# Left queries of two batches gathered in one late stage, keys turned over two PSUM banks, and one pair of heads divided after its product

## The chip, the cores and the metric

The kernel runs on one core of one Trainium2 chip. The metric is the device time of one execution in microseconds (us). The core has five engines that run side by side: TensorE (PE in the profile: matmuls and transposes, results in PSUM), VectorE (DVE), ScalarE (ACT), GpSimd (POOL) and SyncE (SP), whose queue issues nearly all DMAs. PSUM has eight banks of 512 float32 columns on 128 partitions.

## The reference

Eight batches, eight heads, 576 rows, head size 64; then a maxout feed-forward over the 4608 x 512 result. All in float32 (the weights arrive as float64).

```
q_s = exp(q - max over head size);  q_s = q_s / (sum over head size + 1e-9)
k_s = exp(k - max over rows);       k_s = k_s / (sum over rows + 1e-9)
kv  = k_s^T @ v                     # 64 x 64 for each batch and head
a   = q_s @ kv                      # 576 x 64
x   = a of all heads side by side   # 4608 x 512
h   = max(x @ w1, x @ w2, x @ w3)   # 4608 x 768
out = h @ w_out                     # 4608 x 512
```

## The kernel before

**Tiling.** Heads go in pairs (four pairs g per batch, pair number n = 4 b + g), so that two heads fill 128 partitions. Of the 576 rows of a head, 512 are its main rows and 64 are "left"; main rows of one batch make a chunk (c = 0 to 7), and the left rows of all batches together make the ninth chunk (c = 8), whose input is the tile `left`. A float32 product of full precision is made from three fast ones on high and low parts (`wh`, `wl`, `oh`, `ol`, `x` with two halves, `h_h`, `h_l`).

**Weights.** They come as 24 slices of 512 KB (18 for the gates, 6 for w_out). A `Slice` is loaded (L332), its float64 words are joined into float32 by DVE, ACT and POOL (L342 to L359), and split into a high part (L363, ACT) and a low part (L370, DVE or POOL). Four slices are among the first loads. Of the others, every second one from number 8 on is loaded into buffers that open with the event "late".

**Attention, batches 0 and 1 ("turned").** `k_turned` transposes the keys of a pair on PE: four blocks into a tile `pa` (a bank of three), the left block into a quarter of the tile `ps` (one bank, four quarters). DVE takes the maxima of both parts (L450, L451) and their smaller (L452), ACT the exponentials with their sums (L456, L457), PE transposes back (L464, L466), and two copies give `ke` (L473). `k_steps` multiplies keys and values (L511) into a quarter of `ps`, and ACT scales the result into `bdf`, one of two buffers (L527). `q_steps` takes the maxima of ten groups of 64 columns (L550: eight of main rows, two of left rows), then either ten exponentials of 64 columns with their sums (`Q_BY_ACT`, pairs 0 to 6, L567) or one subtraction and one exponential, and scales by the sums (L595). `turned_steps` transposes main rows (L636) and left rows (L640) and copies both to `qf` (L645, L647). `x_steps` multiplies `bdf` by `qf` for main rows and for left rows (L663) and splits the results into high (L666, ACT) and low (L668, DVE).

**Attention, batches 2 to 7.** `k_plain` takes the maximum over rows on GpSimd, the queries are turned by DVE and DMAs, and the products are made in three passes. These start with the event "turn", when all slices are split and batch 1 is done. `x_steps` runs for main and left rows here too.

**Feed-forward.** For each chunk 18 gates (`Chunk.gate`, L693: four column blocks `cc`, one from each pair, three matmuls each), maxima and split (`Chunk.hidden`, L702 to L712), then four output tiles of 18 matmuls (`Chunk.second`, L732). A gate's block `cc` needs x of pair g = cc and one weight slice. The four gate tiles `pf` take half of PSUM.

**Order.** Nothing is looped in plain order: each of these is a generator of steps, each step with an engine, a cost, what it needs and what it frees, and `Streams` plays them against a clock per engine. On an engine it takes, of the steps that could begin, the one of lowest rank, and emits instructions in that order; every engine then runs its own list strictly in order. The ranks come from constants: `AT` and `STEP` (pairs of batches 0 and 1), `FIRST` and `CHUNK` (the later batches), `SLICES_AT`, `SLICE`, `SLICE_STEP`, `SLICE_HI` and `SLICE_LO` (weights), `GATES_AT` (gates). `FIRST_LOADS` spells the first DMAs: w a slice, k, q, v the main rows of the next pair of batch 0, and the capital letters the left rows (the first time those of pair 0, the second time those of pairs 1 to 3). The event "late" is given by

```python
yield Step("-", 0.0, [(x, 0, g) for x in ("x", "xl") for g in range(NP)], gives="late")
```

Of the kernel before, what the change touches and what calls it, by code (L numbers as in the profile page):

```python
# [42 lines left out]
Q_BY_ACT = (0, 1, 2, 3, 4, 5, 6)  # L43
# [6 lines left out]
def dve_reduce(n):  # L50
    return (n + 140) / 960
# [28 lines left out]
class Streams:  # L80
# [88 lines left out]
    def issue(self, t, e, c, s):  # L169
        step = s[4]  # L170
        end = t + c
# [24 lines left out]
def linear_attention_then_maxout_ffn(  # L196
# [49 lines left out]
    pa = ctx.enter_context(tc.tile_pool(name="pa", bufs=3, space=PSUM))  # L246
    ps = ctx.enter_context(tc.tile_pool(name="ps", bufs=1, space=PSUM))
# [16 lines left out]
    q0 = early.tile([P, H, 5, D], F32, name="q0")  # L264
    v0 = early.tile([P, H, 5, D], F32, name="v0")
    bdf = [start.tile([P, P], F32, name=f"bdf{i}", bufs=1) for i in range(2)]
    qbuf = [start.tile([P, 2, 5, D], F32, name=f"q1{i}", bufs=1) for i in range(2)]
# [14 lines left out]
    nc.gpsimd.memset(q0[LEFT:P, :, 4, :], 0.0)  # L282
    for i in range(2):
        nc.gpsimd.memset(bdf[i], 0.0)
    for i in range(2):
        nc.gpsimd.memset(qbuf[i][LEFT:P, :, 4, :], 0.0)
        nc.gpsimd.memset(vbuf[i][:, :, :, D:NV], 1.0)
        nc.gpsimd.memset(vbuf[i][LEFT:P, :, 4, :], 0.0)
# [13 lines left out]
    st = Streams({"pf": 4, "pa": 3, "ps": 4, "keT": 1, "hp": NJ, "tmp": 3, "ke": 2, "qe": 2, "qf": 1, "qt": 2, "tb": 1, "qT": 2, "qhl": 1}, {"pf": in_pf})  # L302
    late_pools, turn_pools = [], []

    quarters = ps.tile([P, 4, P], F32, name="ps")
    small = (quarters[:, i % 4, :] for i in itertools.count())
# [67 lines left out]
    class Pair:  # L374


        def __init__(self, b, g):
            self.b, self.g = b, g
            self.hs = slice(2 * g, 2 * g + 2)
            self.n = b * NP + g  # L380
            self.m = self.n % 2
            self.turned = b < TURNED
            if b == 0:
                self.kt, self.vt, self.qt = k0[:, :, self.hs], v0[:, self.hs], q0[:, self.hs]
            else:
                self.kt, self.vt = kbuf[self.m], vbuf[self.m]
                if self.turned:
                    self.kt = self.kt.rearrange("p h s d -> p (h s d)").rearrange("p (s h d) -> p s h d", s=5, h=2)

# [19 lines left out]
        def v_load(self):  # L409
            if self.b:  # L410
                prev = self.ago("kv") if self.n >= NP + 2 else None
                for hh in range(2):
                    yield Step("S", 0.64, [prev], kb=200)
                    nc.sync.dma_start(out=self.vt[:, hh, 0:4, 0:D], in_=head_rows(v, self.b, 2 * self.g + hh))
# [3 lines left out]
        def q_load(self):  # L418
            if self.b == 0:
                return  # L420
            if self.turned:
                prev = self.ago("qsub") if self.n >= NP + 2 else None
                self.qt = qbuf[self.m]
                yield Step("S", 0.64, [prev], kb=256)
                nc.sync.dma_start(out=self.qt[:, :, 0:4, :], in_=main_rows(q, self.b, self.hs))
                yield Step("S", 0.64, gives=("q", self.n), kb=50)
                nc.sync.dma_start(out=self.qt[0:LEFT, :, 4, :], in_=left_rows(q, self.b, self.hs))
# [6 lines left out]
        def k_turned(self):  # L434

            n, kt = self.n, self.kt
            rooms = [("pa", ("kT", n)), ("ps", ("kTl", n))]
            yield Step("T", 0.6, [("k", n)], take=rooms + [("keT", n)], gives=("ksub", n))
            kT = pa.tile([P, CH], F32, name="pa")
            for s in range(4):  # L440
                nc.tensor.transpose(  # L441
                    out=kT[:, s * P : (s + 1) * P], in_=kt[:, s].rearrange("p h d -> p (h d)"), identity=ident
                )
            kTl = next(small)
            nc.tensor.transpose(
                out=kTl[:, :LEFT], in_=kt[:LEFT, 4].rearrange("p h d -> p (h d)"), identity=ident[:LEFT, :LEFT]
            )
            yield Step("V", dve_reduce(CH) + dve_reduce(LEFT) + 0.13)
            km = att.tile([P, 2], F32, name="km2", bufs=4)
            nc.vector.tensor_reduce(out=km[:, 0:1], in_=kT, op=ALU.max, axis=AX.X, negate=True)  # L450
            nc.vector.tensor_reduce(out=km[:, 1:2], in_=kTl[:, :LEFT], op=ALU.max, axis=AX.X, negate=True)  # L451
            nc.vector.tensor_tensor(out=km[:, 0:1], in0=km[:, 0:1], in1=km[:, 1:2], op=ALU.min)  # L452
            yield Step("A", act(CH) + act(LEFT) + 0.2, free=rooms)
            keT = start.tile([P, S], F32, name="keT", bufs=1)
            ks = self.ks = att.tile([P, 2], F32, name="ks", bufs=4)
            nc.scalar.activation(out=keT[:, :CH], in_=kT, func=AF.Exp, bias=km[:, 0:1], accum_out=ks[:, 0:1])  # L456
            nc.scalar.activation(  # L457
                out=keT[:, CH:], in_=kTl[:, :LEFT], func=AF.Exp, bias=km[:, 0:1], accum_out=ks[:, 1:2]
            )
            rooms = [("pa", ("ke", n)), ("ps", ("kel", n))]  # L460
            yield Step("T", 0.6, take=rooms + [("ke", n)], free=[("keT", n)])
            kep = pa.tile([P, CH], F32, name="pa")
            for s in range(4):
                nc.tensor.transpose(out=kep[:, s * P : (s + 1) * P], in_=keT[:, s * P : (s + 1) * P], identity=ident)  # L464
            kel = next(small)
            nc.tensor.transpose(out=kel[:LEFT, :], in_=keT[:, CH:], identity=ident)  # L466
            e = yield Step("AV", (act(CH) + act(P), dve(CH) + dve(P)), free=rooms)
            ke = self.ke = att.tile([P, 5, 2, D], F32, name="ke")
            for o, i in (
                (ke[:, 0:4].rearrange("p s h d -> p (s h d)"), kep),  # L470
                (ke[:LEFT, 4].rearrange("p h d -> p (h d)"), kel[:LEFT, :]),
            ):
                (nc.scalar.copy if e == "A" else nc.vector.tensor_copy)(out=o, in_=i)  # L473
# [24 lines left out]
        def k_steps(self):  # L498
# [5 lines left out]
                "T", 0.9, [("v", n), self.ago("xmm", 0), self.ago("xmm", 1)], take=last, free=[("ke", n)], gives=("kv", n)  # L504
# [12 lines left out]
            if turned:  # L517
                nc.vector.tensor_scalar(
                    out=rk, in0=self.ks[:, 0:1], scalar1=self.ks[:, 1:2], scalar2=1e-9, op0=ALU.add, op1=ALU.add
                )  # L520
# [4 lines left out]
            for r in heads:  # L525
                to = (bdf if turned else bdh)[self.m]
# [14 lines left out]
        def q_steps(self):  # L541
            n = self.n
            rows = 10 if self.turned else QS
            by_act = n in Q_BY_ACT
            qm = att.tile([P, rows], F32, name=f"qm{rows}", bufs=4)
            qs = att.tile([P, rows], F32, name=f"qs{rows}", bufs=4)
            yield Step("V", dve_reduce(rows * D), [("q", n)])
            if self.turned:
# [4 lines left out]
                if by_act:  # L553
                    yield Step("A", 5 * 0.33, take=[("qe", n)])
# [4 lines left out]
                qe = self.qe = start.tile([P, 5, 2, D], F32, name="qe", bufs=2)  # L559
                rows3 = qe.rearrange("p s h d -> p (s h) d")  # L560
                sums = qs.rearrange("p (s h) -> p s h", h=2)
                if by_act:
                    for hh in range(2):
                        if hh:
                            yield Step("A", 5 * 0.33, gives=("qsub", n))
                        for s in range(5):
                            nc.scalar.activation(  # L567
                                out=qe[:, s, hh, :], in_=src[:, hh, s, :], func=AF.Exp,
                                bias=qm[:, 5 * hh + s : 5 * hh + s + 1], accum_out=sums[:, s, hh : hh + 1],
                            )  # L570
                else:
# [3 lines left out]
                        in1=qm.rearrange("p (h s) -> p h s", h=2).unsqueeze(3).broadcast_to([P, 2, 5, D]),  # L575
                        op=ALU.subtract,
                    )
            else:
# [5 lines left out]
                )  # L584
            if not by_act:
# [4 lines left out]
            yield Step("V", 0.34)  # L590
# [39 lines left out]
        def turned_steps(self):  # L630

            n = self.n
            yield Step("T", 0.5, [("qn", n)], take=[("qf", n), ("pa", ("qT", n)), ("ps", ("qTl", n))], free=[("qe", n)])
            qT = pa.tile([P, CH], F32, name="pa")
            for s in range(4):
# [3 lines left out]
            qTl = next(small)  # L639
            nc.tensor.transpose(  # L640
                out=qTl[:, :LEFT], in_=self.qe[:LEFT, 4].rearrange("p h d -> p (h d)"), identity=ident[:LEFT, :LEFT]
            )
            e = yield Step("AV", (act(CH), dve(CH)), free=[("pa", ("qT", n))])
            qf = start.tile([P, S], F32, name="qf", bufs=1)
            (nc.scalar.copy if e == "A" else nc.vector.tensor_copy)(out=qf[:, :CH], in_=qT)  # L645
            yield Step("A", act(LEFT), free=[("ps", ("qTl", n))], gives=("qhl", n))
            nc.scalar.copy(out=qf[:, CH:], in_=qTl[:, :LEFT])  # L647
            self.terms = [(bdf[self.m], qf)]

        def x_steps(self, u):  # L650
# [4 lines left out]
            cost = f32(w) if self.turned else 3 * f32r(w)  # L655
# [3 lines left out]
            yield Step("T", cost, after, take=[room], gives=("xmm", n, u), free=[("qf" if self.turned else "qhl", n)] if u else ())  # L659
            xT = (next(small) if u else pa.tile([P, CH], F32, name="pa"))[:, :w]  # L660
            last = len(self.terms) - 1
            for i, (l, r) in enumerate(self.terms):
                nc.tensor.matmul(out=xT, lhsT=l, rhs=r[:, cs], start=(i == 0), stop=(i == last))  # L663
# [4 lines left out]
            nc.vector.tensor_sub(out=lo, in0=xT, in1=h.bitcast(F32))  # L668

    class Chunk:
# [6 lines left out]
        def gate(self, j, i):  # L679
            c, js = self.c, slice(j * P, (j + 1) * P)  # L680
            key = (c, j, i)
            for cc in range(NC):
                x = [("x", c, cc)] if c < B else [("xl", b, cc) for b in range(B)]
# [240 lines left out]
```

## Time and profile before

| what | us |
|---|---|
| median of 3 runs | 716.88 (716.74 to 718.5) |
| the profiled execution | 717.27 |
| its span, first to last instruction | 715.5 |
| TensorE busy | 685.4 |
| VectorE, ScalarE, GpSimd busy | 401.7, 254.0, 55.1 |

The span is what the trace covers; the profiled execution's own time is 1.8 us longer. Busy times are shares of the span that an engine spent in instructions. A line of instructions names the line of the kernel (L693), the engine, the operation, output and inputs by tile names, the shapes and the count. "a <- b" in a list of waits means that a stood idle until b was done. PEclk is the clock granted to TensorE as a share of full speed.

### The profile page before, as it was taken

The page shows a single profiled execution, that of the slowest core. Times are in us where ns is not written, and L with a number is a line of the kernel's source. Part 1 is how long each engine was busy: PE and PEld are TensorE (multiplying, and loading weights), DVE is VectorE, ACT ScalarE, POOL GpSimd, SP SyncE. Part 2 cuts the span into 40 slices and gives each one's busy share as a digit, 9 for nine tenths or more (in the row PEclk, how much of TensorE's full clock was granted, in tenths as well). Part 3 has the DMA queues.
Part 4 walks back from the last instruction along what each step waited for, and adds up shares of the span by engine and source line. Part 5 has one row for each costly group of instructions (what it writes and reads, how often), then busy time and mean ns, then how long its engine had stood idle before and what let it go on. Part 6 is the DMA issues. An engine that isn't in the chain of part 4 may idle for free.

```text
span 715.5 us, 9842 instructions
## 1 busy us (share of the span) xinstructions
PE 685.4 (96%) x3528; PEld 552.0 (77%) x3528; DVE 401.7 (56%) x812; ACT 254.0 (36%) x605; POOL 55.1 (8%) x69
## 2 busy tenths in 40 slices
PE   3779899999999999999999999999999999999997
PEld 2457687787888787888888888888888888888885
DVE  6789867388977977865477646653422112211220
ACT  4899745433443425422442234223411111111111
POOL 1222233100010000000000000000000000000000
PEclk9999999999999999999999999999999999999999
DMA  8947423315454334520253015200200010010002
GB/s 222 252 135 231 127 83 106 109 34 129 113 163 122 83 80 110 151 65 17 73 150 86 16 49 164 64 16 28 82 1 0 16 45 0 1 44 16 1 0 60
DMA packets 86417, 58.07 MB, mean 81 GB/s; under 512 B 53344, under 2 KB 77920, under 8 KB 86368
## 3 DMA queue, kind: packets, MB, share of 16 engines
q1 hardware_dynamic: 86288, 57.31, 28.9%
q8 instruction: 28, 0.46, 0.3%
q14 instruction: 21, 0.17, 0.1%
q10 hardware_dynamic: 80, 0.13, 0.0%
HBM read 40.89 MB, written 9.44 MB: 70 GB/s over the span
## 4 chain that ended last, share of the span: by engine, by line
PE 88%; ACT 4%; DVE 4%; DMA 2%; issue 1%; SPq 1%; DVEq 0%; ACTq 0%
PE pf L693 59%; PE pf L732 21%; PE ps L511 3%; PE pa L663 2%; ACT qe L567 2%; PE ps L663 1%; DMA wst<-in_moe_w_dram 1%; ACT keT L456 1%; ACT wst L359 0%; PE pa L464 0%; DMA v<-in_v_dram 0%; DVE m L705 0%; DVE wx L346 0%; PE pa L441 0%; DMA vt<-in_v_dram 0%
## 5 line engine op out<-in xcount | busy, mean ns | idle before, releaser
L693 PE MATMUL pf<-x,wh 128*128 128x512 f32 x1152 | 357.3, 391 | 0.0
L693 PEld LDWEIGHTS pf<-x,wh 128*128 128x128 f32 x1152 | 217.3, 189 | 47.0 <-issue 1.0
L693 PE MATMUL pf<-x,wl 128*128 128x512 f32 x576 | 231.1, 401 | 0.0
L705 DVE TENSOR_TENSOR m<-pf,m 128x512 f32<-128x512 f32 x108 | 74.4, 689 | 180.0 <-PE pf L693 177.5
L693 PEld LDWEIGHTS pf<-x,wl 128*128 128x128 f32 x576 | 108.7, 189 | 23.9 <-issue 0.7
L708 ACT CAST h_h<-m 128x512 fp32r<-128x512 f32 x54 | 33.6, 622 | 191.6 <-DVE m L705 191.4
L732 PE MATMUL pf<-ol,h_h 128*128 128x512 f32 x216 | 88.0, 408 | 0.1
L732 PE MATMUL pf<-oh,h_l 128*128 128x512 f32 x216 | 84.5, 391 | 0.0
L732 PE MATMUL pf<-oh,h_h 128*128 128x512 f32 x216 | 84.3, 390 | 0.0
L702 ACT COPY m<-pf 128x512 f32<-128x512 f32 x54 | 31.7, 587 | 57.8 <-PE pf L693 57.7
L732 PEld LDWEIGHTS pf<-ol,h_h 128*128 128x128 f32 x216 | 40.6, 188 | 9.2 <-DVE ol L370 0.7
L712 DVE TENSOR_TENSOR h_l<-m,h_h 128x512 fp32r<-128x512 f32 x54 | 36.9, 683 | 19.1 <-ACT h_h L708 19.0
L732 PEld LDWEIGHTS pf<-oh,h_l 128*128 128x128 f32 x216 | 40.5, 188 | 9.1
L732 PEld LDWEIGHTS pf<-oh,h_h 128*128 128x128 f32 x216 | 40.6, 188 | 7.6
L693 PE MATMUL pf<-left,wh 128*128 128x512 f32 x144 | 44.4, 389 | 0.0
L486 POOL PARTITION_ALL_REDUCE kma<-km x24 | 18.7, 779 | 299.7 <-DVE ke L489 146.8
L750 ACT COPY m<-pf 128x512 f32<-128x512 f32 x35 | 20.4, 587 | 59.8 <-PE pf L732 54.3
L355 POOL TENSOR_TENSOR wst<-wx,wst 128x512 int32<-128x512 int32 x24 | 31.6, 1318 | 90.9 <-DVE wx L351 55.5
L668 DVE TENSOR_TENSOR x<-pa,x 128x512 fp32r<-128x512 f32 x32 | 22.1, 689 | 29.4 <-ACT x L666 29.3
L600 DVE STREAM_TRANSPOSE tb<-qt 128x576 f32<-128x576 f32 x24 | 30.8, 1282 | 2.4 <-DMA qT<-tb 2.1
L666 ACT CAST x<-pa 128x512 fp32r<-128x512 f32 x32 | 18.7, 585 | 36.1 <-PE pa L663 36.1
L693 PEld LDWEIGHTS pf<-left,wh 128*128 128x128 f32 x144 | 27.0, 188 | 5.7
(114 smaller groups left out, 679.2 us busy)
## 6 DMA issues: line engine op xcount, KB each, us to landing
wst<-in_moe_w_dram SPq DMA_DIRECT2D x18, 512.0 KB, 5.0
out_dram<-m SPq DMA_DIRECT2D x32, 256.0 KB, 2.4
vt<-in_v_dram SPq DMA_DIRECT2D x56, 128.0 KB, 3.0
qt<-in_q_dram SPq DMA_DIRECT2D x24, 288.0 KB, 3.1
qT<-tb SPq DMA_DIRECT2D x192, 36.0 KB, 1.9
kt<-in_k_dram SPq DMA_DIRECT2D x24, 256.0 KB, 3.0
wst<-in_moe_w_out_dram SPq DMA_DIRECT2D x6, 512.0 KB, 3.3
q<-in_q_dram SPq DMA_DIRECT2D x8, 256.0 KB, 4.6
```

The source lines that it names most:

```text
L355: nc.gpsimd.tensor_add(out=low.bitcast(I32), in0=x.bitcast(I32), in1=low.bitcast(I32))
L511: nc.tensor.matmul(out=kv[r, :nv], lhsT=ke[rows, s, hh, :], rhs=self.vt[rows, hh, s, 0:nv], start=(s == 0), stop=(s == 4),)
L600: nc.vector.transpose(out=tb.rearrange("p e (c s) -> p s e c", s=QS), in_=self.qt.rearrange("p s (e c) -> p s e c", e=2))
L663: nc.tensor.matmul(out=xT, lhsT=l, rhs=r[:, cs], start=(i == 0), stop=(i == last))
L668: nc.vector.tensor_sub(out=lo, in0=xT, in1=h.bitcast(F32))
L693: nc.tensor.matmul(out=ps, lhsT=l[:, cc, js], rhs=r, start=(cc == 0 and t == 0), stop=(cc == NC - 1 and t == 2))
L702: nc.scalar.copy(out=m, in_=self.m.pop((j, 0)))
L705: nc.vector.tensor_max(out=m, in0=self.m.pop((j, i)), in1=m)
L708: nc.scalar.copy(out=h, in_=m)
L712: unit[e].tensor_sub(out=lo, in0=m, in1=h.bitcast(F32))
L732: nc.tensor.matmul(out=po, lhsT=l, rhs=r[:, j, :], start=(j == 0 and i == 0), stop=(j == NJ - 1 and i == 2))
L750: nc.scalar.copy(out=o, in_=po)
```

## The change

- Left queries of batches 0 and 1 leave the pairs. Queries of a turned pair are now 8 groups and not 10 (512 columns), without left loads, left transposes, left copies and left products. A new generator, `left_queries`, starts with "turn" and has a rank beside batch 5: two loads of 128 KB, one softmax over 512 columns, four transposes, a copy, eight products of 64 columns with the eight matrices, one split into `left`.
- `bdf` keeps a matrix for each of the eight pairs, where two buffers were used in turn; the product of keys and values of these pairs no longer waits for x of two pairs before.
- PSUM: `pa` (three banks) and `ps` (one) become one tile of four banks. A wide piece is 640 columns, all of one bank and a quarter of the next (two of them); the small pieces are the other three quarters of the second and fourth bank (six).
- Keys of a turned pair are transposed into one wide piece: one maximum and one exponential over 576 columns, one copy over 640 columns back.
- Pair 2 (`Q_AFTER`): its queries are not divided before the product. One subtraction and one exponential; four transposes; for each block a product with a two-column 0/1 tile `of_head` gives the sums and one with `bdf` gives the rows; DVE divides; four transposes turn the result. Pair 6 goes from ten exponentials by ACT to a subtraction, one exponential and a sum.
- "late" and "turn" wait for x of main rows alone.
- The planner takes a TensorE step that begins before 34 us as 1.85 times as long (`COLD`), and the constants of the ranks and the first loads are others. `GATES_AT` is 1000, so that all attention goes ahead of gates on TensorE.
- GpSimd sets up `keT`'s end, `of_head` and the eight matrices at the start; `vbuf` is set at "turn".

```diff
+COLD = 34.0, 1.85
-FIRST, CHUNK, SLICE = 21.0, 39.5, 0.35
-AT = (16.0, 6.9, 25.7, 26.2, 99.1, 87.2, 114.2, 74.5)
-STEP = (0.38, 3.02)
-SLICES_AT, SLICE_STEP, SLICE_HI, SLICE_LO = -30.5, 2.83, 6.78, 0.26
-GATES_AT = 50.0
-FIRST_LOADS = 'qwQKkKqvVvwQkkwqVkwqvv'
+FIRST, CHUNK, SLICE = 148.8, 39.5, 0.88
+AT = (60.4, 14.9, 48.7, 69.3, 94.8, 78.9, 168.8, 74.1)
+STEP = (0.05, 4.42)
+SLICES_AT, SLICE_STEP, SLICE_HI, SLICE_LO = -27.9, 0.34, 0.31, 0.11
+GATES_AT = 1000.0
+FIRST_LOADS = 'wkwKkqKwvvkqqkvwvqVV'
-Q_BY_ACT = (0, 1, 2, 3, 4, 5, 6)
+Q_BY_ACT = (0, 1, 3, 4, 5)
+Q_AFTER = (2,)
...
+        if e == "T" and t < COLD[0]:
+            c *= COLD[1]
...
-    pa = ctx.enter_context(tc.tile_pool(name="pa", bufs=3, space=PSUM))
-    ps = ctx.enter_context(tc.tile_pool(name="ps", bufs=1, space=PSUM))
+    pa = ctx.enter_context(tc.tile_pool(name="pa", bufs=1, space=PSUM))
...
+    banks = pa.tile([P, 2, 2 * CH], F32, name="pa")
+    wide = (banks[:, i % 2, 0 : 5 * P] for i in itertools.count())
+    small = (banks[:, i % 2, (5 + i // 2 % 3) * P : (6 + i // 2 % 3) * P] for i in itertools.count())
...
+            km = att.tile([P, 1], F32, name="km1", bufs=4)
+            nc.vector.tensor_reduce(out=km, in_=kT[:, :S], op=ALU.max, axis=AX.X, negate=True)
...
+            nc.scalar.activation(out=keT[:, :S], in_=kT[:, :S], func=AF.Exp, bias=km, accum_out=ks)
...
+            copy(out=ke.rearrange("p s h d -> p (s h d)"), in_=kep)
...
+            room, sums_room = [("pa", ("xn", n))], [("ps", ("xs", n))]
+            yield Step("T", 1.2, [("bd", n)], take=room + sums_room, free=[("qf", n)])
+            xn, sums = next(wide)[:, :CH], next(small)
+            for s in range(4):
+                l = qf[:, s * P : (s + 1) * P]
+                nc.tensor.matmul(out=sums[:, 2 * s : 2 * s + 2], lhsT=l, rhs=of_head, start=True, stop=True)
+                nc.tensor.matmul(out=xn[:, s * P : (s + 1) * P], lhsT=l, rhs=bdf[:, n], start=True, stop=True)
...
+    def left_queries():
+        yield Step("S", 0.64, ["turn"], take=[("qt", "left")], kb=128)
+        qt = turn_pools[0].tile([P, QS, D], F32, name="qt", bufs=2)
+        ql = qt[:, 0:H, :]
+        nc.sync.dma_start(out=ql[0:LEFT], in_=left_rows(q, 0, slice(0, H)))
...
+        for n in range(TURNED * NP):
+            b, g = divmod(n, NP)
+            at = g * P + b * LEFT
+            nc.tensor.matmul(out=xT[:, at : at + LEFT], lhsT=bdf[:, n], rhs=qT[:, at : at + LEFT], start=True, stop=True)
...
-        yield Step("-", 0.0, [(x, 0, g) for x in ("x", "xl") for g in range(NP)], gives="late")
+        yield Step("-", 0.0, [("x", 0, g) for g in range(NP)], gives="late")
...
+    st.add(left_queries(), FIRST + CHUNK * 4)
```

More of the change, by code (lines that the diff above doesn't have):

```diff
@@ L281, in linear_attention_then_maxout_ffn @@
         )
[L282 to L288, printed above, removed]
+    nc.gpsimd.memset(keT[:, S:], 0.0)
+    nc.gpsimd.memset(of_head, 0.0)
+    for h, r in enumerate(heads):
+        nc.gpsimd.memset(of_head[r, h : h + 1], 1.0)
+    nc.gpsimd.memset(bdf, 0.0)
     def main_rows(src, b, hs):
@@ L436, in k_turned @@
             n, kt = self.n, self.kt
[L437 to L440, printed above, removed]
+            room = [("pa", ("kT", n))]
+            yield Step("T", 0.6, [("k", n)], take=room + [("keT", n)], gives=("ksub", n))
+            kT = next(wide)
+            for s in range(5):
+                rows = P if s < 4 else LEFT
@@ L451, in k_turned @@
[L451 to L463, printed above, removed]
+                    out=kT[:, s * P : s * P + rows], in_=kt[:rows, s].rearrange("p h d -> p (h d)"),
+                    identity=ident[:rows, :rows],
+                )
@@ L464, in k_turned @@
+            kep = next(wide)
+            for s in range(5):
                 nc.tensor.transpose(out=kep[:, s * P : (s + 1) * P], in_=keT[:, s * P : (s + 1) * P], identity=ident)
-            kel = next(small)
-            nc.tensor.transpose(out=kel[:LEFT, :], in_=keT[:, CH:], identity=ident)
-            e = yield Step("AV", (act(CH) + act(P), dve(CH) + dve(P)), free=rooms)
+            e = yield Step("AV", (act(5 * P), dve(5 * P)), free=room)
             ke = self.ke = att.tile([P, 5, 2, D], F32, name="ke")
[L469 to L473, printed above, removed]
+            copy = nc.scalar.copy if e == "A" else nc.vector.tensor_copy
@@ L503, in k_steps @@
             yield Step(
-                "T", 0.9, [("v", n), self.ago("xmm", 0), self.ago("xmm", 1)], take=last, free=[("ke", n)], gives=("kv", n)
+                "T", 0.9, [("v", n), *([] if turned else [self.ago("xmm", u) for u in range(2) if n - 2 >= TURNED * NP or u == 0])], take=last, free=[("ke", n)], gives=("kv", n)
             )
@@ L542, in q_steps @@
             n = self.n
-            rows = 10 if self.turned else QS
+            rows = 8 if self.turned else QS
             by_act = n in Q_BY_ACT
+            self.after = self.turned and n in Q_AFTER
             qm = att.tile([P, rows], F32, name=f"qm{rows}", bufs=4)
@@ L584, in q_steps @@
                 )
+            if self.after:
+                yield Step("A", act(rows * D), gives=("qn", n))
+                nc.scalar.activation(out=rows3, in_=rows3, func=AF.Exp)
+                return
             if not by_act:
@@ L632, in turned_steps @@
             n = self.n
-            yield Step("T", 0.5, [("qn", n)], take=[("qf", n), ("pa", ("qT", n)), ("ps", ("qTl", n))], free=[("qe", n)])
-            qT = pa.tile([P, CH], F32, name="pa")
+            room = [("pa", ("qT", n))]
+            yield Step("T", 0.5, [("qn", n)], take=[("qf", n), *room], free=[("qe", n)])
+            qT = next(wide)[:, :CH]
             for s in range(4):
@@ L654, in x_steps @@
             room = ("ps" if u else "pa", ("x", u, n))
-            cost = f32(w) if self.turned else 3 * f32r(w)
+            after_sums = self.turned and n in Q_AFTER
+            cost = 0.5 if after_sums else f32(w) if self.turned else 3 * f32r(w)
+            freed = ("qe", ("xn", n)) if after_sums else ("qf" if self.turned else "qhl", n)
             after = [("bd", n), ("qhl", n), ("xmm", n, 0) if u else None]
@@ L658, in x_steps @@
                 after += [("gates", b - 2) if b >= 2 else None, "late" if b == 1 else None]
[L659 to L663, printed above, removed]
+            yield Step("T", cost, after, take=[room], gives=("xmm", n, u), free=[freed] if u or self.turned else ())
+            xT = next(small if u else wide)[:, :w]
+            if after_sums:
+                for s in range(4):
+                    nc.tensor.transpose(
+                        out=xT[:, s * P : (s + 1) * P], in_=self.xr[:, 2 * s : 2 * s + 2].rearrange("p r d -> p (r d)"),
+                        identity=ident,
+                    )
+            else:
+                last = len(self.terms) - 1
+                for i, (l, r) in enumerate(self.terms):
+                    nc.tensor.matmul(out=xT, lhsT=l, rhs=r[:, cs], start=(i == 0), stop=(i == last))
             h, lo = self.x_place(u)
```

124 lines of the change are left out of this document (81 added, 43 removed).

## The prediction

> **What bounds the kernel now.** I read the page first, then the busy time by windows, the waits of TensorE, and the timelines of the first 130 us.
>
> ```profile
> span 715.5 us, 9842 instructions
> PE 685.4 (96%) x3528; PEld 552.0 (77%) x3528; DVE 401.7 (56%) x812; ACT 254.0 (36%) x605; POOL 55.1 (8%) x69
> PE   3779899999999999999999999999999999999997
> ```
>
> TensorE (PE) is busy in 685.4 of 715.5 us, so 30.1 us are idle, and the third row shows where: the digits under 9 are in the first five slices (89 us) and the last. The windows say it more exactly (busy us and instructions of PE, its weight loads, DVE, ACT, POOL; granted clock, DMA share, GB/s).
>
> ```profile
> 0.00:8.43 8.43, 0.00 (x1) 0.04 (x1) 4.38 (x18) 2.16 (x3) 2.12 (x13) 1.00 0.71 196
> 8.43:30.00 21.57, 13.82 (x77) 9.31 (x78) 16.68 (x38) 16.49 (x70) 3.86 (x3) 1.00 1.07 263
> 30.00:58.00 28.00, 22.63 (x132) 16.19 (x131) 23.36 (x58) 26.18 (x104) 7.78 (x6) 1.00 0.49 137
> 58.00:73.40 15.40, 14.63 (x81) 12.08 (x82) 14.19 (x33) 12.87 (x39) 2.64 (x3) 1.00 0.95 288
> 73.40:84.20 10.80, 8.56 (x54) 5.88 (x53) 9.74 (x22) 8.34 (x29) 3.87 (x3) 0.84 0.40 110
> 84.20:100.00 15.80, 15.80 (x71) 13.08 (x70) 11.70 (x24) 10.19 (x26) 4.70 (x4) 1.00 0.29 94
> ```
>
> PE idles 8.43 us before the first keys land, 7.75 us to 30, 5.37 us to 58, and 0.77 and 2.24 us in the next two windows: 24.6 us. From 84 us on it is full. In 30 to 58 us ScalarE (ACT) is busy 26.18 of 28 us and VectorE (DVE) 23.36: they carry four pairs' softmax and the splitting of the weights, and PE waits for both.
>
> Two marks divide this stage. At 58 us the last x of batch 0 is there. At 82.4 us the ninth gate begins.
>
> ```profile
> 57.29 0.69 DVE L668 TENSOR_TENSOR x<-pa,x 128x512 fp32r<-128x512 f32 x1 [0.37 <-ACT x L666]
> 60.98 0.22 DVE L668 TENSOR_TENSOR left<-ps,left 128x64 fp32r<-128x64 f32 x1
> 62.15 2.42 SPq L332 DMA_DIRECT2D wst<-in_moe_w_dram  x4
> 82.36 0.79 PE L693 MATMUL pf<-x,wl 128*128 128x512 f32 x1
> ```
> ```profile
> 30.00:58.00 28.00, 11.65 (x36) 6.98 (x36) 1.00 0.49 137
> 58.00:73.40 15.40, 13.76 (x60) 11.19 (x60) 1.00 0.95 288
> ```
>
> The second fence is the gates' line alone: 36 matmuls before 58 us, 60 after, together eight gates of twelve. The ninth needs weight slice 8, whose load waits for "late": all x and left columns of batch 0, which end at 61.20, 3.2 us after the last x. It goes out only then (62.15).
>
> Part of PE's early waits is of another kind:
>
> ```profile
> PE pa L441 <- DMA k<-in_k_dram: 8.4, 1, 8.4
> PE ps L511 <- DVE km L451: 2.5, 2, 1.5
> PE ps L663 <- ACT keT L457: 1.6, 1, 1.6
> ```
>
> Tile ps is one bank with four quarters. L511 writes the product of keys and values, yet waits for a reduction of another quarter: matmuls into that bank wait for readers of any part of it.
>
> **The change part by part.** *ScalarE's work on a pair of batches 0 and 1.*
>
> ```profile
> 12.60 1.65 ACT qe L567 x10
> L456 ACT ACTIVATE keT<-pa,km 128x512 f32<-128x512 f32 x5 | 3.4, 679 | 0.2 <-DVE km L452 0.2
> L457 ACT ACTIVATE keT<-ps,km 128x64 f32<-128x64 f32 x5 | 1.5, 303 | 0.0
> L473 ACT COPY ke<-ps 64x128 f32<-64x128 f32 x3 | 0.8, 264 | 0.0
> L647 ACT COPY qf<-ps 128x64 f32<-128x64 f32 x4 | 0.8, 212 | 0.2
> L666 ACT CAST left<-ps 128x64 fp32r<-128x64 f32 x3 | 0.6, 210 | 2.2 <-DVE wx L347 2.2
> ```
>
> Five query exponentials with their read-outs take 1.65 us, 0.33 each; eight in place of ten save 0.66. The keys' second exponential (0.30) goes and the first grows by 64 columns (0.05, by the slope between 303 and 679 ns): 0.25. One copy of 640 columns for 512 and 128: 0.15. The two left copies go: 0.2 each, less some overlap. That is 1.3 us a pair, 5.2 for batch 0. Pair 2 (Q_AFTER) does one exponential of 512 columns (0.68 by the nearest row) for eight: 2.0 more. One and a half pairs of batch 1 also fall before 58 us: 1.0. Together 8.2 us of ACT before that mark.
>
> *VectorE's work.*
>
> ```profile
> L550 DVE TENSOR_REDUCE qm<-q 128x10 f32<-128x640 f32 x6 | 4.8, 810 | 0.0
> L450 DVE TENSOR_REDUCE km<-pa 128x1 f32<-128x512 f32 x6 | 4.1, 676 | 0.4 <-PE pa L441 0.4
> L595 DVE TENSOR_TENSOR qe<-qe,qs 128x640 f32<-128x640 f32 x4 | 3.3, 819 | 0.0
> L451 DVE TENSOR_REDUCE km<-ps 128x1 f32<-128x64 f32 x5 | 1.1, 220 | 0.7 <-PE ps L511 0.5 <-ACT qf L647 0.2
> L668 DVE TENSOR_TENSOR left<-ps,left 128x64 fp32r<-128x64 f32 x3 | 0.7, 223 | 1.2 <-ACT keT L457 0.6 <-ACT wst L359 0.5
> ```
>
> Queries' maximum and scaling fall from 640 to 512 columns: 0.13 each, by 810 against 676. One reduction of 576 columns for two and a minimum: at least 0.35. The left subtraction: 0.22. So 0.85 a pair, 3.4 for batch 0, less 0.69 for the subtraction that pair 2 now needs: 2.7 us.
>
> *What the first stage gains.* From 8.43 to 58 us ACT is busy 42.67 us and DVE 40.04. If each kept its share of the time, ACT's 34.5 us would need 40.1 (9.5 less) and DVE's 37.3 would need 46.2 (3.4 less). DVE becomes the scarcer one, so I stay nearer its end, and add something for the bank: the small tiles now lie in two banks, and per pair only the product of keys and values uses them, where five tiles did. I take 5.5 us; ends 0 (weights, which rank ahead of attention, take all that is freed) and 9.5. PE's own work fits: 36.45 us busy in 49.6, less some 3 for left transposes and products, in 44. Two wide rooms replace three; each is held for a few us a pair, which the pace of one x in about seven us leaves hidden. Without that slack each room held adds itself to the chain.
>
> *The late slices.* "late" no longer waits for left columns: 3.2 us less from last x to slice 8. The stall that it ends costs 2.24 us of idling plus a slow clock behind it:
>
> ```profile
> 80.80:84.20 3.40, 3.34 (x10) 0.50 0.73 206
> 17.73 1.11 PE L441 MATMUL pa<-ident,k 128*128 128x128 f32 x4
> 33.11 0.78 PE L693 MATMUL pf<-x,wl 128*128 128x512 f32 x1
> 36.88 0.39 PE L693 MATMUL pf<-x,wl 128*128 128x512 f32 x1
> 39.53 0.61 PE L636 MATMUL pa<-ident,qe 128*128 128x128 f32 x4
> ```
>
> Half clock over 3.34 us busy loses 1.7. I take 3.0 of the 3.9; ends 0 and 3.9.
>
> *Where PE is full.* Left queries of batches 0 and 1 now come once, in the full stage: four transposes and eight products.
>
> ```profile
> 120.42 0.60 PE L636 MATMUL pa<-ident,qe 128*128 128x128 f32 x4
> 48.94 0.33 PE L663 MATMUL ps<-qf,bdf 128*128 128x64 f32 x2
> ```
>
> 0.60 + 8 x 0.33 = 3.2 us exposed. Left out of the full stage are the left products and transposes of some two pairs of batch 1, 0.5 each: net +2.2 (ends +0.6, if the products pipeline, and +3.2). Their DVE and ACT work lies under gates; were that cover gone it would cost about 5 us. Pair 2's eight small products and second transposes (about +1 us of PE) fall where PE idles. Six small query loads leave SP's early queue and two join it late, with nobody behind in a hurry. POOL's larger memset ends before its first weight addition; the memsets moved to the turn stand ahead of an idle queue. The waits of the key product on older x go: no wait row names them, so nothing. Ranks and GATES_AT change the order; I price that in the rivals.
>
> Sum against the profiled execution (717.27 us, 1.8 outside its span): 717.27 - 5.5 - 3.0 + 2.2 = 711.0. The runs' median is 716.88, 0.4 lower: **710.6**. By the ends: 704 to 720.
>
> **A rule on the clock.** The granted clock reads 1.00 through the start, but four transposes take 1.11 us at 17.73 and 0.61 at 39.53: PE runs at half speed until about 36.8, 3.7 us after the gates began. The Trainium skill, "TensorE: Matmul & The Clock Gate", Part 1, says that the clock opens after a window of about 3.4 us of sustained work; the trace agrees. Its Part 4 adds that transposes don't count as such work, and the half clock behind 73.4 to 82 us, a stretch of transposes and short waits, fits. By that rule more such stretches make this change smaller; the third rival works it out from rows.
>
> **The rivals.**
>
> *Values too late (slower).* FIRST_LOADS moves both left loads of v to the very end, and the key product of a pair needs them.
>
> ```profile
> 14.93 1.53 PE L511 MATMUL ps<-v,ke 128*64 128x64 f32 x20 [1.25 <-ACT ke L473]
> 27.11 1.53 PE L511 MATMUL ps<-v,ke 128*64 128x64 f32 x20 [1.45 <-DVE km L451]
> 19.26 0.98 SPq L791 DMA_DIRECT2D v<-in_v_dram  x2
> v<-in_v_dram SPq DMA_DIRECT2D x4, 256.0 KB, 4.9
> ```
>
> The last loads go out near 20 us and land 4.9 later, so no such product starts before 25, where the first ran at 14.93. Three pairs took from 27.11 to 57.98, 10.3 us a pair; four pairs at 9.3 (1.0 saved) end at 62.3, 4.3 later than now: 717.27 + 4.3 - 3.0 + 2.2 = 720.8. It decides if a pair takes over 8.4 us from 25 on; my forecast needs 6.9. Against it: keys, queries and slices can be prepared before 25, though ke has two buffers.
>
> *The freed time goes to the weights (same).* x comes no earlier, half the stall goes: 717.27 - 1.5 + 2.2 = 718, in the runs' terms 717.6. For it: DVE is 83% busy in 30 to 58 us, and slices rank first.
>
> *A colder PE (same).* With GATES_AT at 1000 attention goes ahead of gates on PE, so stretches of transposes grow. Three more at 1.4 us: 711.0 + 4.2 = 715.2, or 714.8.
>
> **How the numbers follow.** The forecast has 0.60, late values 0.16, the weights 0.16, the cold clock 0.08. A difference under 0.3% (2.2 us) is about what can't be told from none. Faster 0.62 (the forecast and a little of the rivals), same 0.21, slower 0.17. The forecast's own range is 704.5 to 714.5; with the rivals, leaving out about 0.2, mostly above, 704.5 to 719.0.
>
> **What would show it.** Right: the last x of batch 0 near 52 us; ACT's early share falling more than DVE's; four loads out within 1.5 us of that x; no matmul into a small tile waiting for a key reduction; about 3 us of left products and transposes beyond 250 us with PE full. Wrong: first key product and first x so late that few gates precede the last x; PE idling over 22 us before 84; transposes at 1.1 us after 40.

## The result and the profile after

The changed kernel takes 744.02 us (742.19 to 748.69) against 717.24 us: a ratio of 1.0381, 95% interval 1.0326 to 1.0435. The prediction, 710.6 with a range to 719.0, was wrong in sign as well as in size. One execution of 1378.97 us and one of 773.2 stand apart in the last two runs described below, and are left out of the figures of those runs.

From the page of the changed kernel (742.33 us, 1.8 of them outside the span):

```profile
span 740.5 us, 9764 instructions
PE 693.0 (94%) x3542; PEld 552.0 (75%) x3542; DVE 400.8 (54%) x793; ACT 245.5 (33%) x515; POOL 54.5 (7%) x69
PE   2577999899999999999999999999999999999997
```

The span grew by 25.0 us. TensorE idles 740.5 - 693.0 = 47.5 us, where it idled 30.1: 17.4 us more. It is also busy 7.6 us longer, with 14 instructions more. ScalarE is busy 8.5 us less, so the relief that was meant is there; the time is not.

Two windows of each kernel divide the idling (same columns as in the prediction). First before, then after:

```profile
0.00:160.00 160.00, 135.35 (x721) 103.62 (x722) 119.23 (x262) 103.26 (x320) 37.84 (x47) 0.99 0.51 144
160.00:600.00 440.00, 439.12 (x2322) 357.13 (x2321) 261.32 (x520) 134.80 (x258) 17.25 (x22) 1.00 0.27 75
```
```profile
0.00:160.00 160.00, 125.97 (x657) 95.36 (x658) 108.55 (x221) 88.63 (x221) 36.88 (x46) 0.99 0.49 140
160.00:600.00 440.00, 430.96 (x2290) 344.73 (x2289) 266.89 (x536) 136.70 (x260) 17.59 (x23) 1.00 0.28 75
```

In the first 160 us PE idles 34.0 us instead of 24.65: 9.4 more. In the 440 us behind, where the kernel before was full, it idles 9.04 instead of 0.88: 8.2 more. That second number is the surprise, since nothing the prediction discussed could stop PE there except two microseconds of left queries. TensorE's waits in that stretch name the place, before and after:

```profile
PE ps L663 <- DVE bdl L531: 0.9, 2, 0.6
```
```profile
PE pa L682 <- DVE x L687: 8.2, 9, 1.3
PE pa L682 <- DVE bdl L524: 0.6, 1, 0.6
```

Nine times PE waits at the product of queries and matrix (L682) for VectorE's subtraction that makes the low part of x (L687). One of the nine in the timeline of the changed kernel (start, duration):

```profile
189.92 0.40 PE L682 MATMUL pa<-q_h,bdh 128*128 128x512 f32 x1
190.36 0.59 ACT L685 CAST x<-pa 128x512 fp32r<-128x512 f32 x1 [2.29 <-PE pa L682]
192.05 0.68 DVE L687 TENSOR_TENSOR x<-pa,x 128x512 fp32r<-128x512 f32 x1
192.78 0.30 PE L682 MATMUL pa<-q_l,bdh 128*128 128x64 f32 x1 [1.09 <-DVE x L687]
```

The main product of a pair ends at 190.32 in a wide piece, columns 0 to 511 of the tile: its first bank. The left product of the same pair goes to a small piece, columns 1664 to 1727: its fourth bank. It needs nothing from the subtraction and shares no bank with it, and still starts only when the subtraction has read the first bank (192.05 + 0.68). The gates behind it on PE wait too. In the kernel before, the same two products, in tiles of their own:

```profile
170.02 0.40 PE L663 MATMUL pa<-q_h,bdh 128*128 128x512 f32 x1
171.62 0.19 PE L663 MATMUL ps<-q_l,bdh 128*128 128x64 f32 x1
```

The left product stands there without a bracket: it waited for nobody.

The early stage shows the same in the other direction, an engine that reads waiting for PE:

```profile
32.33 1.41 PE L450 MATMUL pa<-ident,k 128*128 128x128 f32 x5 [0.72 <-ACT bdf L520]
35.17 2.08 PE L682 MATMUL pa<-qf,bdf 128*128 128x512 f32 x2 [1.43 <-ACT bdf L520]
37.28 0.76 DVE L456 TENSOR_REDUCE km<-pa 128x1 f32<-128x576 f32 x1 [5.60 <-PE pa L682]
```

The keys of a pair lie transposed in the third and fourth bank at 33.74. Their maximum (L456) begins at 37.28, when PE has ended a product into the first bank. VectorE stood idle for 5.60 us, 3.5 of them after its data was there, in a stage where the prediction called it the scarcer engine.

So x comes late, and with it the gates. First and last x of batch 0, and the first gates:

```profile
42.68 0.69 DVE L687 TENSOR_TENSOR x<-pa,x 128x512 fp32r<-128x512 f32 x1 [1.33 <-ACT qf L639]
67.85 0.69 DVE L687 TENSOR_TENSOR x<-pa,x 128x512 fp32r<-128x512 f32 x1 [2.06 <-PE pa L450]
47.20 0.78 PE L760 MATMUL pf<-x,wl 128*128 128x512 f32 x1
49.05 1.05 PE L760 MATMUL pf<-x,wh 128*128 128x512 f32 x2
50.34 0.63 PE L760 MATMUL pf<-x,wh 128*128 128x512 f32 x2
```

In the kernel before, the first two gate matmuls at that speed:

```profile
36.41 0.64 PE L693 MATMUL pf<-x,wh 128*128 128x512 f32 x2
```

The last x is at 67.85 where it was at 57.29. Two gate matmuls take 1.05 us at half speed and 0.63 at full speed, and full speed begins at 50.34 where it began at 36.41. So PE works at half speed for 14 us longer, one reason for its longer busy time. Later it falls back once more:

```profile
140.62 1.13 PE L682 MATMUL pa<-qf,bdf 128*128 128x512 f32 x2 [1.47 <-ACT qf L639]
142.42 0.76 PE L760 MATMUL pf<-x,wl 128*128 128x512 f32 x1 [0.68 <-ACT x L685]
144.37 1.05 PE L635 MATMUL pa<-ident,qe 128*128 128x128 f32 x4
```

Four transposes take 1.05 us again, behind waits of 1.47 and 0.68 us. The granted clock from 120 to 160 us reads 0.96, which hides this: from 142.40 to 146.20 it is 0.55. The Trainium skill, "TensorE: Matmul & The Clock Gate", Part 1, has the clock open after a window of about 3.4 us of sustained work. The trace agrees: 3.1 us pass from the first gate (47.20) to full speed (50.34), with transposes right ahead of them.

### The profile page after: what moved, and what is told of

Its sections match the earlier page's. It is cut to its first block, busy times and chain, and to the rows that moved or that the text cites. A ratio compares the mean times of both kernels' runs of the same rounds, so it can differ in the third digit from the quotient of the medians.

```text
span 740.5 us, 9764 instructions
## 1 busy us (share of the span) xinstructions
PE 693.0 (94%) x3542; PEld 552.0 (75%) x3542; DVE 400.8 (54%) x793; ACT 245.5 (33%) x515; POOL 54.5 (7%) x69
## 4 chain that ended last, share of the span: by engine, by line
PE 87%; DVE 6%; ACT 3%; DMA 2%; issue 1%; SPq 0%; POOL 0%; DVEq 0%; ACTq 0%
PE pf L760 57%; PE pf L799 20%; PE pa L682 5%; PE pa L506 4%; DVE x L687 1%; ACT x L685 1%; DMA wst<-in_moe_w_dram 1%; PE pa L635 1%; PE pa L464 1%; DVE bdl L524 1%; DMA v<-in_v_dram 1%; ACT qe L561 1%; DVE tb L598 0%; PE pa L450 0%; DVE qs L587 0%
## 5 line engine op out<-in xcount | busy, mean ns | idle before, releaser
L779 DVE TENSOR_TENSOR h_l<-m,h_h 128x512 fp32r<-128x512 f32 x54 | 39.3, 728 | 19.6 <-ACT h_h L775 19.5
L687 DVE TENSOR_TENSOR x<-pa,x 128x512 fp32r<-128x512 f32 x32 | 22.0, 687 | 35.7 <-ACT x L685 22.2
L363 POOL TENSOR_TENSOR wst<-wx,wst 128x512 int32<-128x512 int32 x24 | 31.7, 1321 | 99.0 <-DVE wx L359 34.3
```

Source lines behind the costliest of these rows:

```text
L363: nc.gpsimd.tensor_add(out=low.bitcast(I32), in0=x.bitcast(I32), in1=low.bitcast(I32))
L779: unit[e].tensor_sub(out=lo, in0=m, in1=h.bitcast(F32))
```

## The experiments

The theory: in this program TensorE's writes into a PSUM *tile* and the other engines' reads of it are kept in the order in which they were emitted, whichever of its banks they touch. Making `pa` and `ps` one tile of four banks therefore extended to four banks the waits that only `ps` had. Rivals: the bank itself is contended; the new order (ranks, first loads, attention ahead of gates) is bad; the moved work (left queries, pair 2) costs more than it saves.

**The same banks as two tiles** (the changed kernel).

```diff
-    pa = ctx.enter_context(tc.tile_pool(name="pa", bufs=1, space=PSUM))
+    pa = ctx.enter_context(tc.tile_pool(name="pa", bufs=2, space=PSUM))
-    banks = pa.tile([P, 2, 2 * CH], F32, name="pa")
-    wide = (banks[:, i % 2, 0 : 5 * P] for i in itertools.count())
-    small = (banks[:, i % 2, (5 + i // 2 % 3) * P : (6 + i // 2 % 3) * P] for i in itertools.count())
+    banks = [pa.tile([P, 2 * CH], F32, name="pa") for _ in range(2)]
+    wide = (banks[i % 2][:, 0 : 5 * P] for i in itertools.count())
+    small = (banks[i % 2][:, (5 + i // 2 % 3) * P : (6 + i // 2 % 3) * P] for i in itertools.count())
```

> The changed kernel with its four banks as two tiles of two banks (a wide piece and its three small pieces each), nothing else touched. Theory T (one tile): engines that touch the same PSUM tile wait for each other in the order of emission, whatever bank they touch, and the change put everything but the gates into one tile. Then half of the pairs of accesses come free: 10 to 18 of the 27 us come back, 726 to 734 us, and the waits of the x products for the subtraction of x (8.2 us after 110 us) fall to under half. Theory P (plan): the new ranks, loads and the late left queries cost the time; then nothing moves, 740 to 746 us.

Measured: 722.33 us, ratio to the kernel before 1.0057 (1.0035 to 1.0079), 21.7 us under the changed kernel, more than the 10 to 18 that were expected. Every engine has the same instructions in the same order, with pieces of the same size in the same turn; only the division into tiles differs. Its windows, then the pair whose left product waited above, then the pair that follows it:

```profile
0.00:160.00 160.00, 132.49 (x726) 101.44 (x727) 117.93 (x242) 92.35 (x229) 37.64 (x47) 0.97 0.51 146
160.00:600.00 440.00, 439.83 (x2309) 355.67 (x2309) 261.14 (x519) 135.40 (x258) 16.89 (x22) 1.00 0.28 74
```
```profile
181.27 0.40 PE L682 MATMUL pa<-q_h,bdh 128*128 128x512 f32 x1
182.78 0.69 DVE L687 TENSOR_TENSOR x<-pa,x 128x512 fp32r<-128x512 f32 x1
182.88 0.19 PE L682 MATMUL pa<-q_l,bdh 128*128 128x64 f32 x1
```
```profile
190.81 0.40 PE L682 MATMUL pa<-q_h,bdh 128*128 128x512 f32 x1
191.87 0.69 DVE L687 TENSOR_TENSOR x<-pa,x 128x512 fp32r<-128x512 f32 x1
192.61 0.30 PE L682 MATMUL pa<-q_l,bdh 128*128 128x64 f32 x1
```

The first pair's pieces now lie in two tiles, and its left product begins at 182.88, while the subtraction still runs. The second pair's pieces lie in one tile, in its two banks, and its left product begins 0.05 us after the subtraction has ended (191.87 + 0.69).

This holds for all pairs. Batches 2 to 7 have 24 left products, each in another bank than the main product of its pair. In the changed kernel 19 of them begin 0.05 or 0.06 us after the end of the subtraction. Pieces are handed out in a fixed turn, so their tiles can be counted off: 11 of these 19 have both pieces in one tile in the two-tile run, and all 11 still begin 0.05 us after it. The other 8 have them in two tiles, and all 8 begin before it ends. So the unit of the wait is the tile, inside a single run too. The 11 waits that are left cost next to nothing, since the gates ahead of them fill the time.

Idling in the full stage is 0.17 us instead of 9.04, and in the first 160 us 27.5 instead of 34.0. Of the 20.3 us of span won back, 15.4 are idling; 4.9 are busy time of the same 3542 matmuls, whose first gates at full speed stand at 44.05 instead of 50.34. The order alone and the moved work alone are out as causes of these 21.7 us.

**The kernel before with its four banks joined**, nothing else changed.

```diff
-    quarters = ps.tile([P, 4, P], F32, name="ps")
-    small = (quarters[:, i % 4, :] for i in itertools.count())
+    banks = pa.tile([P, 4, CH], F32, name="pa")
+    wide = (banks[:, i % 3, :] for i in itertools.count())
+    small = (banks[:, 3, i % 4 * P : (i % 4 + 1) * P] for i in itertools.count())
```

> The kernel before, with its three tiles pa and the tile ps made one tile of four banks: same pieces, same rooms, same order of instructions. Theory T: slower by 12 to 30 us, 729 to 747 us, with TensorE waits for readers of other banks that the kernel before does not have, and an idle time of TensorE above 40 us. Theory P: no change, 716 to 719 us.

Measured: 751.57 us, 1.0465 (1.0442 to 1.0488): 33.6 us from the join alone, in the same order of instructions, and more than the 12 to 30 that were expected. Its full stage and TensorE's waits there:

```profile
160.00:600.00 440.00, 430.11 (x2272) 342.49 (x2271) 271.61 (x542) 137.22 (x262) 18.70 (x24) 1.00 0.27 73
PE pa L663 <- DVE x L668: 7.7, 9, 1.3
```

Nine waits of the left product, as in the changed kernel, in a kernel that has no other part of the change. With the two-tile run this shows it from both sides: cut the tile and most of the loss goes, join it and the loss comes. The bank can't be the cause either, since the main product (one of three banks) and the left one (the fourth) are in different banks here throughout.

**The tile join under the other order.** The changed kernel with the ranks, first loads and `COLD` of the kernel before, once as one tile and once as two.

```diff
-COLD = 34.0, 1.85
+COLD = 0.0, 1.85
-FIRST, CHUNK, SLICE = 148.8, 39.5, 0.88
+FIRST, CHUNK, SLICE = 21.0, 39.5, 0.35
-GATES_AT = 1000.0
+GATES_AT = 50.0
...
-FIRST_LOADS = 'wkwKkqKwvvkqqkvwvqVV'
+FIRST_LOADS = 'qwKkKqvVvwkkwqVkwqvv'
```

> The changed kernel with the ranks, the order of first loads and the cold factor of before (without the loads of left queries): the order of steps goes back, the one tile stays. Theory T: still slow, 733 to 748 us, with the same waits of the x products after 110 us. Theory P: 714 to 722 us.

> The changed kernel with two PSUM tiles of two banks and with ranks, order of first loads and cold factor of before. If the rest of the loss of the two-tile version (4.4 us) is the new order of loads and ranks, this gives 712 to 718 us, with the first x near 30 us and the clock open before 38 us. If it is the tiles that are still shared, it stays at 720 us or goes above it.

Measured: 754.5 us (1.0503, 1.0475 to 1.0531) as one tile, 728.22 (1.0151, 1.013 to 1.0172) as two. The one-tile run is slower than the 733 to 748 us that were expected. The two-tile run is outside 712 to 718 us, so the 4.4 us that two tiles still lost are not the price of the new order. The join costs 26.3 us in this order too. The new constants are not what made the change slow: on the changed work they are better than the old ones, by 10.5 us as one tile and by 5.9 as two.

**The changed work in the old tiles.** Three tiles `pa`, the bank `ps` and the key turning of the kernel before; left queries late; pair 2 like the others.

```diff
+    pa = ctx.enter_context(tc.tile_pool(name="pa", bufs=3, space=PSUM))
+    ps = ctx.enter_context(tc.tile_pool(name="ps", bufs=1, space=PSUM))
+    quarters = ps.tile([P, 4, P], F32, name="ps")
+    small = (quarters[:, i % 4, :] for i in itertools.count())
+    wide = (pa.tile([P, CH], F32, name="pa") for _ in itertools.count())
...
-Q_BY_ACT = (0, 1, 3, 4, 5)
-Q_AFTER = (2,)
+Q_BY_ACT = (0, 1, 2, 3, 4, 5)
+Q_AFTER = ()
```

> The changed kernel with the PSUM tiles of before (three of one bank, one of four quarters) and with the keys of before (left part in a quarter of its own, two maxima, two exponentials, two copies); pair 2 is treated as the other pairs are. Ranks, loads, left queries and matrices stay those of the change. Theory T: the whole loss goes, 706 to 722 us, with no wait of a product for a reader in another bank in the steady part. Theory P: 735 us or more.

Measured: 718.69 us, 1.0011 (0.9994 to 1.0027): no difference from the kernel before. Against the changed kernel 25 us are back, and the expected gain is missing all the same. The stage that was to give it, its last x of batch 0, and PE's longest waits:

```profile
8.43:58.00 49.57, 29.98 (x180) 21.72 (x180) 38.30 (x89) 34.69 (x128) 12.65 (x10) 0.86 0.71 191
63.49 0.68 DVE L702 TENSOR_TENSOR x<-pa,x 128x512 fp32r<-128x512 f32 x1
PE pa L472 <- ACT keT L464: 15.6, 5, 6.8
```

In the kernel before, ACT was busy 42.66 us of that window and DVE 40.04. Here they are busy 34.69 and 38.30, and x is 6.2 us later, so a part of their work has only moved behind 58 us. PE's longest waits are for ScalarE's key exponentials (five times, 15.6 us). The span of the profiled execution is 715.5 us, as before: PE is 4.2 us less busy in it (681.2) and 4.2 us more idle (34.3).

**Left queries late, alone.** The tiles, keys, ranks and pairs of the kernel before; its first loads, less those of left queries.

```diff
-COLD = 34.0, 1.85
+COLD = 0.0, 1.85
...
-Q_BY_ACT = (0, 1, 2, 3, 4, 5)
+Q_BY_ACT = (0, 1, 2, 3, 4, 5, 6)
```

(The diff is against the kernel with the old tiles; the ranks and first loads change as in the pair of runs above.)

> One part of the change alone: PSUM tiles, keys, ranks, order of first loads and the treatment of all pairs are those of before, but left queries of batches 0 and 1 come once in the late stage, bdf has a matrix for each pair, and the two events wait for x of main rows alone. Theory A (ScalarE and VectorE bound the first stage): less work there brings x of batch 0 forward by 2 to 5 us and the late slices with it; 711 to 716 us. Theory B (the order and the waits bound it, not the work): the freed time is not used and the late products stand in the full stage; 717 to 722 us.

Measured: 724.03 us, 1.0083 (1.0056 to 1.0111), slower than both theories had it, with less work ahead of x. First and last x of batch 0 come at 27.48 and 59.85; before, they came at 30.24 and 57.29. TensorE's waits show new entries for weights and for a key copy:

```profile
PE ps L454 <- DVE ke L481: 3.0, 1, 3.0
PE pf L775 <- DVE wl L379: 2.0, 3, 1.5
PE pf L814 <- DVE ol L379: 1.8, 1, 1.8
```

What moved work is worth depends on the order that the planner then finds. Which of its steps costs the 6 us was not singled out.

**The first loads** (the old tiles, with the kernel before's order of loads).

```diff
-FIRST_LOADS = 'wkwKkqKwvvkqqkvwvqVV'
+FIRST_LOADS = 'qwKkKqvVvwkkwqVkwqvv'
```

> The version with the PSUM tiles and keys of before and all else of the change (718.7 us), but with the first loads in the order of before: left values early again. Theory V (values too late): the first product of keys and values moves from 27 to about 15 us, first x to 31 us, the clock opens before 38 us, and 3 to 7 us come back: 711 to 716 us. Theory W (the loads are not what binds): within 2 us of 718.7.

Measured: 716.92 us, 0.9988 (0.9977 to 0.9999), 1.8 us under the run with late values. The window, and the last x of batch 0:

```profile
8.43:58.00 49.57, 35.88 (x220) 23.99 (x219) 38.65 (x94) 40.37 (x152) 11.87 (x10) 0.93 0.72 197
61.03 0.68 DVE L702 TENSOR_TENSOR x<-pa,x 128x512 fp32r<-128x512 f32 x1
```

What theory V names does come: the first product of keys and values is at 15.17, the first x at 26.98, and the first gates run at full speed (0.63 us for two at 28.55). The last x comes 2.5 us earlier than in the run with late values, and PE is 5.9 us busier in the window. Of the 3 to 7 us that this was to give, 1.8 are there, little more than the noise. The last x is still 3.7 us later than in the kernel before, at an equal time, so it does not set the end by itself.

**All of the change, but tiles that are apart.** The two wide pieces are tiles of two banks each, the small ones quarters of a bank of their own, and the gates give up one of their four tiles.

```diff
-    pf = ctx.enter_context(tc.tile_pool(name="pf", bufs=4, space=PSUM))
-    pa = ctx.enter_context(tc.tile_pool(name="pa", bufs=1, space=PSUM))
+    pf = ctx.enter_context(tc.tile_pool(name="pf", bufs=3, space=PSUM))
+    pa = ctx.enter_context(tc.tile_pool(name="pa", bufs=2, space=PSUM))
+    ps = ctx.enter_context(tc.tile_pool(name="ps", bufs=1, space=PSUM))
```

> The changed kernel with the pieces apart: two tiles of two banks for wide pieces alone, one bank with four quarters for the small ones, and three gate tiles in place of four. All of the change's savings stay. If sharing of tiles is the whole loss and three gate tiles suffice: 712 to 720 us. If three gate tiles starve TensorE in the full stage, idle time after 160 us rises by more than 5 us and the time is 725 us or more.

Measured: 717.67 us, 0.9997 (0.9986 to 1.0009). The first stage, and the last x of batch 0:

```profile
8.43:58.00 49.57, 30.89 (x185) 22.22 (x186) 36.20 (x78) 34.43 (x113) 12.65 (x10) 0.93 0.73 196
59.75 0.69 DVE L689 TENSOR_TENSOR x<-pa,x 128x512 fp32r<-128x512 f32 x1
```

All that the change was to save is saved in this run, ACT and DVE are less busy than before, and the last x still comes 2.5 us later. Keys over two banks and the undivided pair 2 cost nothing that shows when their tiles are apart, and bring nothing. The run with two tiles, in which small pieces still share a tile with wide ones, had 1.0057; taking them out (and a gate tile away) brings that back.

**Other ranks on the old tiles.** Two sets, each with an end 2 to 3 us earlier in the kernel's own plan.

```diff
-COLD = 34.0, 1.85
+COLD = 40.0, 1.85
-AT = (60.4, 14.9, 48.7, 69.3, 94.8, 78.9, 168.8, 74.1)
-STEP = (0.05, 4.42)
-SLICES_AT, SLICE_STEP, SLICE_HI, SLICE_LO = -27.9, 0.34, 0.31, 0.11
-FIRST_LOADS = 'wkwKkqKwvvkqqkvwvqVV'
+AT = (60.4, 14.9, 42.8, 75.4, 98.5, 123.5, 159.2, 74.6)
+STEP = (1.7, 0.29)
+SLICES_AT, SLICE_STEP, SLICE_HI, SLICE_LO = -34.6, 0.25, 1.24, 3.12
+FIRST_LOADS = 'wkwKkqKwvvkqqvkvwqVV'
-Q_BY_ACT = (0, 1, 2, 3, 4, 5)
+Q_BY_ACT = (1, 2, 3, 4, 5, 6)
```

(This is the second set, with `SLICE` 0.89 for 0.88; the first moves every rank, the first loads, and `Q_BY_ACT` to all eight.)

> The kernel with one-bank tiles and before's keys (18.69 us over 700 in its run, 718.69), with other ranks, other first loads and ten exponentials on ScalarE for every pair; in the kernel's own plan its last TensorE step ends some 3 us sooner. Theory (with tiles apart the order is what is left to gain, and the plan holds): 714 to 717. Rival (the plan misses as much as it gains, since the first stage runs on waits that it doesn't know): 717 to 721.

> As the other, with ranks near those of the run of 718.69 us: the last pairs of batch 0 and the slices moved by a few places, the first loads by one, 2 to 3 us sooner in the plan. Theory: 714 to 717. Rival: 717 to 721. If one of the two gains and the other not, the plan's end doesn't tell what the chip does to a few us.

Measured: the first 716.26 us, 0.9984 (0.9972 to 0.9996), in the band that was expected; the second 714.03 us (five executions, 712.95 to 717.0), 0.9953 (0.9937 to 0.9968), at the lower end of its band. The second is faster than both kernels, 0.5% under the one before. Its profiled execution took 717.0, above the median, so its rows show the order rather than the gain:

```profile
0.00:160.00 160.00, 133.28 (x725) 103.20 (x726) 123.19 (x267) 97.22 (x266) 40.43 (x49) 0.98 0.53 149
61.21 0.68 DVE L702 TENSOR_TENSOR x<-pa,x 128x512 fp32r<-128x512 f32 x1
```

PE idles 26.7 us in the first 160 where the same work in the changed kernel's order idled 29.6 (715.5 - 681.2 = 34.3 us in the whole span). The last x of batch 0 is again later than before's.

## Why the prediction was wrong

**The step that failed first: "add something for the bank: the small tiles now lie in two banks".** The prediction had the row, 2.5 us of "L511 <- DVE km L451", and read it as a wait of the bank. It is one of the tile. By the bank, six small pieces in two banks are a relief, and that was put into the 5.5 us. By the tile, all wide and small pieces become neighbours, and what `ps` alone showed holds for everything that passes through `pa`. The row fitted both readings, because `ps` was one tile and one bank, and the prediction did not ask which of the two it was; the listing of the change shows one `pa.tile` of four banks. Its sign, "no matmul into a small tile waiting for a key reduction", holds to the letter and tells nothing: in place of that wait stand others of the same kind, the left products' for subtractions in another bank (8.2 us) above all. Price: 21.7 us in the changed kernel's order, 26.3 in the old one, 33.6 in the kernel before. No rival had it.

The Trainium skill, "PSUM — Partial Sum Buffer", section "PSUM bank collisions raise a hardware error", says to guard PSUM by bank and quadrant, or simply by bank. The waits measured here are coarser than that: a bank's reader held up a writer of another bank, at the cost above.

**The step that failed second: the first stage's gain of 5.5 us.** With tiles apart it is absent (1.0011, 0.9988, 0.9997). The step that failed is "if each kept its share of the time": it took engines that are 86% and 81% busy for bounds. With all of the change and its tiles apart, ACT and DVE are 69% and 73% busy in the window, and x comes 2.5 us later instead of 5.5 earlier. ACT is 8.2 us less busy there, the very size that was worked out, but by luck: x is later, so a part of the work has moved behind the mark. With the old first loads the shares are 81% and 78%, and x comes 3.7 us later. There the time goes to other work: the first three x of batch 1 come at 69.37, 79.45 and 85.57, where the first two came at 79.99 and 126.52. That the engines are links of a row of waits fits these runs, but is argued and not shown. The bound "0" of that term was the right end; whether the weights take the time, as its reason had it, was not tested.

**The late slices (3.0 us).** Not settled alone. In the changed kernel no wait of PE for a slice stands out where the stall was; its waits there are for PSUM. Of the loads of slices around the last x (67.85 to 68.54), three go out from 67.68 to 69.20, within the 1.5 us that the sign named, and the next at 71.47, outside them; x itself was late.

**Left queries in the full stage (+2.2 net).** The right size:

```profile
L717 PE MATMUL pa<-ident,qt 128*128 128x128 f32 x4 | 0.6, 272 | 0.0
L729 PE MATMUL pa<-qT,bdf 128*128 128x64 f32 x16 | 1.9, 271 | 0.0
```

Four transposes and the products take 2.5 us, with 3.2 predicted; the products are sixteen instructions and not eight, and overlap.

**The rival of late values.** Its fact held, and its price did not. The first product of keys and values:

```profile
27.36 0.91 PE L506 MATMUL pa<-v,ke 128*64 128x64 f32 x12 [1.45 <-ACT qf L639]
```

It is at 27.36 where it was at 14.93, and in the old tiles, without the wait, at 24.35, near the 25 of the prediction. But there early values give back 1.8 us, not the 9.8 between 720.8 and the forecast's 711.0.

**The rival of a colder PE.** True as a fact (50.34 for 36.41, and the fall back at 142), but in good part an effect of the waits: with two tiles the same order has gates at full speed from 44.05, and its granted clock from 120 to 160 us reads 1.00. The rival's 1.4 us a stretch has no row behind it. The signs that the prediction named for being wrong, PE idle for over 22 us early and transposes at 1.1 us after 40, are both in the trace: 19.87, 7.46 and 4.38 us of idling in the first three windows of 30 us, and 1.05 at 144.37. The first sign tells little, since the kernel before idles 24.6 us up to 84 us.

**What stays open.** What holds the first stage back once the tiles are apart, why moving left queries out costs 6 us in the old order, and which of the ranks wins the 0.5%.

## What to carry to other kernels

In a kernel built like this one, cut PSUM into as many tiles as there are independent users; a tile that spans banks to gain layout (one wide read, spare quarters) chains TensorE to every engine that reads any of it, also in stages that the change wasn't about. When a profile shows an engine waiting for a reader of data it doesn't need, find out whether the unit of the wait is the bank or the tile before predicting what a new layout does. And before crediting a relief of two busy engines, ask whether one of them is full or both may be links of a row of waits: here less work on both gave nothing in three runs with tiles apart, and 0.5% with one of two other orders.

## What the runs showed that was not expected

- The unit of waiting on PSUM was the tile: the same instructions in the same order took 744.02 us with one tile of four banks and 722.33 with two of two, and 717.96 against 751.57 in the kernel before. Inside the two-tile run the 11 pairs with both pieces in one tile wait, and the 8 with pieces in two tiles don't.
- Waits of about 1 us, nine in 440 us, cost 8.2 us of a stage in which TensorE is otherwise idle for 0.2 to 0.9.
- Waits early lengthen TensorE's busy time too: the same 3542 matmuls were busy 693.0 us as one tile and 688.1 as two.
- With three gate tiles in place of four TensorE idles 0.02 us from 160 to 600 us, so the missing tile costs nothing there.
